# An attention and bilinear FFN block: PSUM banks of the first odd tiles and last down products, values of complete key tiles within the first FFN tile, two reads of plain down products exchanged

## The chip, the cores and the metric

The kernel runs on one core of a Trainium2 chip, in one launch. The metric is the device time of an execution in microseconds; lower is better. TensorE (PE) multiplies into PSUM, eight banks of 128 partitions x 512 fp32; VectorE (DVE) and ScalarE (ACT) read PSUM; GpSimd (POOL) works on SBUF; SyncE's queue (SP) issues the DMAs. Each engine runs its instructions in the order in which the program lists them, and waits on semaphores where it needs another's result.

## The reference

One transformer block in fp32 over 2048 tokens of width 576, with 32 query heads of 18 that share one key and one value head, and an FFN of width 4608 without a nonlinearity:

```python
x = A_x
h = x + _A_ref(_layernorm(x, axis=-1), A_wq, A_wk, A_wv, A_wo)    # softmax(q k^T / sqrt(18)) v, then wo
h2 = h + _B_ref(_layernorm(h, axis=-1), B_w_gate, B_w_up, B_w_down)  # ((x W) * (x V)) W2
```

## The kernel before, in words

**Tiling.** Tokens lie in four blocks b of 512 (NB = 4). Attention works in score pairs (`pair`, L674): two products of keys and queries fill a two-bank PSUM tile "s", ACT takes the exponential into an SBUF tile P (L702). Two pairs complete a key tile of 128 keys; its P tiles wait in the list `pend` until `flush` (L709) multiplies them with V into an accumulator (`values`, L704). In the trace a value product is two PE instructions, so a key tile is eight instructions at L706. 32 pairs make a group of four heads, eight groups a block.

**The FFN.** `ffn(b)` (L1062) runs over 36 tiles f of 128 columns, numbered n_ = 36 b + f. A tile has 27 steps j, nine chunks c of X by three combinations of high and low parts; each step is a gate product into pg and an up product into pu (L1091), in the two halves of the PE array. Behind the steps ACT copies pg into hf (L1125) and DVE multiplies pu into it (L1129). While attention of later blocks is left over (`on`, all of FFN blocks 0 and 1 and the first tiles of block 2), score pairs are dealt among the steps by lists (`PAIRS`, `FIRST` for f = 1, `ENTRY` for n_ = 0: before which step a pair stands), and two more pairs follow an even tile's steps. Behind an even tile, all complete key tiles are flushed and the accumulator is closed: DVE saves it to SBUF (`save`, L719), or turns it when its group is done (L732). Later in the same even tile, from f = 2, comes a down product (`down`, L993) of the pair of tiles before. Block 2's last tiles run without pairs ("off", f from 21); their gate and up banks lie in "s" tiles.

**PSUM.** Tag "s" has two tiles of two banks; "f" has two banks that are taken in turn; "m" and "a" have one bank each. "a" holds the accumulator of the values in the FFN. A new tile on a bank waits for the last reader of the one before. An odd tile usually takes pg in "a" and pu in "f", an even tile pg in "f" and pu in "m"; f = 1 is an exception before, with pg in "f" and pu in "m", and so is the last tile of a block, with pg in "f".

**Down products.** Most pairs of tiles use a seven-product scheme in 14 stages of three matmuls (128 x 288). A stage accumulates onto its bank, and its sum is added into the residual h, either by DVE straight from PSUM (L1045) or by an ACT copy into one of three `tmp` buffers (L1049) that POOL adds (L1050). A later stage on the same bank waits for the read of the one before. `STAGES` is the list while attention is on, `WIDE` the one without it, with four banks. The weights of the next tile are split in the middle of a wide product: DVE's part (L963) stands behind stage 6's read. The last pair of a block (17) has eight plain products y (L1005) of six matmuls each; in blocks 0 and 1 their banks come from `ps_y`, and products with n = 0 are read by DVE (L1015), those with n = 1 by ACT (L1012) and POOL.

**Between blocks.** `spread(b)` transposes the normalised h of the next block (L935), splits it (ACT L940, DVE L941) and copies rows between partition halves by DMA (`X<-X`, L944) for chunks 5 to 8, which steps 15 to 26 read. `both` alternates it with the last down product. SP's queue carries the weights of tiles (`wr`, L953), of down products (`wdo`, L970), the sums' operands and all stores.

Of the kernel before, what the change touches and what calls it, by code (L numbers as in the profile page):

```python
# [57 lines left out]
class Block:  # L58
# [17 lines left out]
        return self.ps.tile([P, TB], F32, tag="m", bufs=1, name=name)  # L76

    def ps_y(self, i, name):
        return self.ps_f(name) if i % 3 else self.ps_m(name)

    def ps_r(self, name):
        self.n_ring += 1
# [979 lines left out]
    def ffn(self, b):  # L1062
        pe, act, dve = self.pe, self.act, self.dve
        X, hid, todo = self.X, [], None
        ahead = self.ahead()
        if b == 0:
            self.sums = self.weight_sums()
            next(self.sums)
        for f in range(NF):
            n_ = NF * b + f  # L1070
            k = f % 2
            w = self.ws.pop(n_)
            on = self.on = self.more(b + 2)
            self.cast_left = self.nc.gpsimd.tensor_copy if on else act.copy
            last = f == NF - 1 and b + 1 < NB
            end = b == NB - 2
            if on:
                pg = (self.ps_a if k and not last and f > 1 else self.ps_f)(f"pg{n_}")
                pu = (self.ps_f if k and f > 1 else self.ps_m)(f"pu{n_}")
            else:  # L1080
                gu = self.ps_s(f"gu{n_}")
                pg, pu = gu[:, 0], gu[:, 1]
            j = 0
            at = FIRST if f == 1 else ENTRY if n_ == 0 else PAIRS[2] if last else PAIRS[k]
            for c in range(9):
                for wk, xk in ((0, 0), (0, 1), (1, 0)):
                    for _ in range(at.count(j)):
                        if on and self.more(b + 2):
                            self.pair()
                    for o, ps in ((0, pg), (64, pu)):  # L1090
                        pe.matmul(ps, w[o:o + 64, wk, c], X[o:o + 64, xk, c], start=(j == 0), stop=(j == 26))  # L1091
                    if j == (8 if on else 2) and todo and not plain(n_ - 2):
                        self.left_sums()
                    if j == (3 if on else 9 if k else 27):
                        self.split_w(n_ + 1)
                    if j == 3 and not on and not k:
                        self.split_w(n_ + 1, (0,))
                    if j == (14 if on else 9 if k else 27):
                        self.load_w(n_ + 2)
                    if j == 5 and k:  # L1100
                        self.left_first(n_ - 1, hid[0])
                    if j == 6 and not k:
                        self.split_wo()
                    if j == (12 if k else 18):
                        self.run_aux(within=True, wo=False)
                    if 0 < f < NF - 1 and j in (8, 16, 24) and self.sums:
                        if next(self.sums, "end") == "end":
                            self.sums = None
                            self.load_wd(self.n_wd + 2)
                    if j == 6 and last and not end:  # L1110
                        self.normal(b + 1)
                    if end and f == TURN - 2 and j == 12:
                        self.normed[NB - 1] = self.mv, self.rstd(self.mv[:, :, 1], "bl", self.nc.gpsimd)
                    if end and f in AHEAD and j in AHEAD[f]:
                        for _ in range(AHEAD[f][j]):
                            next(ahead)
                    j += 1
            if todo and not on:
                for i, _ in enumerate(self.down(b, *todo)):
                    if i == 6:  # L1120
                        self.split_w(n_ + 1, (1,))
                        self.load_w(n_ + 2)
                self.load_wd(self.n_wd + 7)
            hf = self.hh.tile([P, TB], F32, tag="hf", bufs=2, name=f"hf{n_}")
            act.copy(hf, pg)  # L1125
            for _ in range(2 if on and not k else 0):
                if self.more(b + 2):
                    self.pair()
            dve.tensor_tensor(hf, pu, hf, ALU.mult)  # L1129
            hid.append(hf)  # L1130
            if k:
                self.left(n_ - 1, hid)
                hid = []
            if end and f in TURNS:
                for _ in range(TURNS[f]):
                    next(ahead)
            if not k or last:
                self.flush(len(self.pend), True)
            if todo and on:
                for i, _ in enumerate(self.down(b, *todo)):  # L1140
                    if i == 3:
                        self.saved()
                self.load_wd(self.n_wd + 7)
            self.saved()
            if f < NF - 1:
                self.run_aux(wo=k)
            todo = (f // 2,) if k else None
        if end:
            del X, pg, pu, gu, w, ps, hf, self.X
            self.last_block(ahead, self.down(b, *todo))  # L1150
            return
        both(self.spread(b + 1), self.down(b, *todo))
        self.load_wd(self.n_wd + 4)
        if b + 2 < NB:
            self.load_x(b + 2)
# [388 lines left out]
    def run(self):  # L1544
# [105 lines left out]
P1, P2, P3, P4, P5, P6, P7 = (0, 0), (1, 1), (6, 2), (2, 6), (3, 3), (4, 4), (5, 5)  # L1650
# [24 lines left out]
WIDE = [(0, 0, P1, True, (0, 0), False), (1, 2, P1, True, (0, 0), False), (0, 1, P5, True, (1, 1), True),  # L1675
        (1, 3, P5, True, (1, 1), False), (0, 0, P6, False, (0, 1), True), (1, 2, P6, False, (0, 1), False),
        (0, 1, P3, False, (0, 1), True), (1, 3, P3, False, (0, 1), False), (0, 0, P7, False, (1, 1), False),
        (1, 2, P7, False, (1, 1), False), (0, 1, P2, True, (0, 0), True), (1, 3, P2, True, (0, 0), True),
        (0, 0, P4, False, (1, 0), True), (1, 2, P4, False, (1, 0), True)]
LOW, HIGH = [0, 2, 4, 6, 8, 1, 3, 5, 7], [1, 3, 5, 7, 8, 0, 2, 4, 6]  # L1680

# [1 line left out]
def both(a, b):  # L1683

    live = [a, b]
    while live:
        live = [x for x in live if next(x, drain) is not drain]


def plain(n):  # L1690

    return n % NF == NF - 2
# [116 lines left out]
```

## Time and profile before

| what | value |
|---|---|
| three runs | 2266.13, 2270.27, 2272.32 us; median 2270.27 |
| the profiled execution | 2268.11 us, its span 2266.3 us |
| mean granted TensorE clock | 0.998 |
| busiest after PE (share of the span) | PE weight loads 72%, ACT 63%, DVE 61%, POOL 40% |

In the rows of an engine's timeline the first two numbers are start and duration in us, and brackets at the end hold the idle time before and who ended it. Rows of waits have the total in us, the number of times and the longest. A row of windows has a stretch, its length, the busy time (and instructions) of PE, PE weight loads, DVE, ACT and POOL, then the granted clock, the share of the DMA engines and GB/s.

### The profile page before, as it was taken

To read this page: it belongs to the slowest core of one execution; us is meant where nothing else is said; L and a number is where in the kernel's file an instruction comes from. 1 tells how busy PE (TensorE), PEld (TensorE's weight loads), DVE (VectorE), ACT (ScalarE), POOL (GpSimd) and SP (SyncE) were. 2 spreads that over 40 slices of the span, in tenths; PEclk is the share of its full clock that TensorE was granted. 3 is DMA by queue.
4 is the path that set the end of the run, shared out by engine and by line. 5 is a ranking of instruction groups with operands and counts; after the bars stand their busy time and mean duration, and the time that the engine had idled before them with its cause. 6 is when DMAs were issued, how large, how long until landed. Compare 5 with 4: busy or idle time off the path is not lost.

```text
span 2266.3 us, 45964 instructions
## 1 busy us (share of the span) xinstructions
PE 2229.2 (98%) x17972; PEld 1638.3 (72%) x17972; DVE 1371.3 (61%) x2213; ACT 1432.1 (63%) x1941; POOL 897.0 (40%) x972
## 2 busy tenths in 40 slices
PE   7999999999999999999999999999999999999999
PEld 5333345777777777677777777767777788999999
DVE  8565644565556556455555556546455667788776
ACT  7888877656666666566665666665666534555553
POOL 4455401444344444244444435433332454322222
PEclk9999999999999999999999999999999999999999
DMA  5879843455455555555455554564333445677775
GB/s 174 272 256 299 290 138 105 153 171 164 155 168 169 161 183 159 166 158 172 150 173 170 171 160 165 165 201 143 111 123 105 131 162 193 209 244 237 235 249 175
DMA packets 200498, 407.01 MB, mean 180 GB/s; under 512 B 22446, under 2 KB 54318, under 8 KB 200278
## 3 DMA queue, kind: packets, MB, share of 16 engines
q1 hardware_dynamic: 197685, 393.42, 54.2%
q0 software_dynamic: 2592, 10.62, 1.5%
q8 instruction: 143, 2.34, 0.4%
q14 instruction: 78, 0.63, 0.1%
HBM read 317.27 MB, written 74.55 MB: 173 GB/s over the span
## 4 chain that ended last, share of the span: by engine, by line
PE 78%; DMA 2%; DVE 2%; POOL 2%; issue 1%; ACT 1%; SPq 1%; POOLq 0%; ACTq 0%; DVEq 0%
PE pg L1091 19%; PE acc L706 15%; PE y L1039 12%; PE s L701 9%; PE gs L1318 8%; PE pu L1091 5%; PE yq L1283 4%; PE yo L880 3%; PE gs L1325 1%; DMA wr<-in_wgu_dram 1%; POOL h L1050 1%; PE gu L1091 1%; DMA X<-X 1%; DVE ws L963 0%; PE y L1005 0%
## 5 line engine op out<-in xcount | busy, mean ns | idle before, releaser
L702 ACT ACTIVATE P<-s 128x1024 f32<-128x1024 f32 x1024 | 1009.9, 1028 | 229.6 <-PE s L701 145.7
L1091 PE MATMUL pu<-X,ws 64*128 64x512 f32 x2511 | 683.5, 390 | 11.1 <-DVE hf L1129 7.7
L1091 PE MATMUL pg<-X,ws 64*128 64x512 f32 x2511 | 682.8, 390 | 0.0
L1091 PEld LDWEIGHTS pg<-X,ws 64*128 64x128 f32 x2511 | 466.3, 186 | 69.3 <-DMA X<-X 0.9
L1091 PEld LDWEIGHTS pu<-X,ws 64*128 64x128 f32 x2511 | 465.9, 186 | 27.5 <-DVE hf L1129 8.9
L706 PE MATMUL acc<-P,V 128*32 128x512 f32 x4096 | 479.1, 598 | 0.0
L701 PE MATMUL s<-q,kT 56*128 56x512 f32 x2048 | 430.7, 415 | 4.8 <-ACT P L702 3.9
L1050 POOL TENSOR_TENSOR h<-h,tmp 128x288 f32<-128x288 f32 x313 | 251.5, 833 | 331.9 <-ACT tmp L1049 330.0
L1049 ACT COPY tmp<-y 128x288 f32<-128x288 f32 x313 | 125.1, 400 | 342.3 <-PE y L1039 307.4
L701 PEld LDWEIGHTS s<-q,kT 56*128 56x128 f32 x2048 | 201.7, 184 | 170.4 <-ACT P L702 122.2
L1039 PEld LDWEIGHTS y<-wdo,room 128*128 128x128 f32 x2142 | 289.9, 188 | 43.9 <-issue 38.5
L1039 PE MATMUL y<-wdo,room 128*128 128x288 f32 x2142 | 303.8, 300 | 2.4 <-ACT tmp L1049 2.1
L706 PEld LDWEIGHTS acc<-P,V 128*32 128x32 f32 x4096 | 114.6, 109 | 254.8 <-issue 252.0
L1045 DVE TENSOR_TENSOR h<-h,y 128x288 f32<-128x288 f32 x401 | 172.7, 453 | 191.4 <-PE y L1039 191.4
L963 DVE TENSOR_TENSOR ws<-wr,ws 128x1152 fp32r<-128x1152 f32 x108 | 188.6, 1746 | 108.7 <-POOL ws L960 107.3
L1129 DVE TENSOR_TENSOR hf<-pu,hf 128x512 f32<-128x512 f32 x93 | 63.7, 685 | 226.9 <-ACT hf L1125 226.9
L960 POOL CAST ws<-wr 128x1152 fp32r<-128x1152 f32 x108 | 130.8, 1212 | 153.3 <-DMA wr<-in_wgu_dram 136.2
L96 POOL CAST room<-hf 128x256 fp32r<-128x256 f32 (+1 forms) x92 | 58.3, 634 | 320.0 <-DVE hf L1129 320.0
L1266 POOL TENSOR_TENSOR wsum<-wsum,wsum 128x512 f32<-128x512 f32 x72 | 146.3, 2032 | 42.5 <-DMA wsum<-in_wgs_dram 37.0
L1091 PE MATMUL gu<-X,ws 64*128 64x512 f32 x810 | 94.5, 389 | 0.0
L97 DVE TENSOR_TENSOR room<-hf,room 128x256 fp32r<-128x256 f32 (+1 forms) x108 | 91.9, 851 | 3.4 <-ACT room L96 1.9
L1091 PEld LDWEIGHTS gu<-X,ws 64*128 64x128 f32 x810 | 78.3, 184 | 13.9 <-issue 0.7
(268 smaller groups left out, 2762.4 us busy)
## 6 DMA issues: line engine op xcount, KB each, us to landing
wdo<-wd_dram SPq DMA_DIRECT2D x492, 288.0 KB
wr<-in_wgu_dram SPq DMA_DIRECT2D x108, 576.0 KB
wsum<-in_wgs_dram SPq DMA_DIRECT2D x108, 256.0 KB
wd_dram<-wd_room SPq DMA_DIRECT2D x20, 1008.0 KB
wsum_dram<-wsum SPq DMA_DIRECT2D x72, 256.0 KB
raw<-wsum_dram SPq DMA_DIRECT2D x72, 256.0 KB
q<-q_dram SPq DMA_DIRECT2D x64, 216.0 KB
raw<-in_wgs_dram SPq DMA_DIRECT2D x54, 256.0 KB
```

The lines of the kernel that those rows point to most:

```text
L701: self.pe.matmul(s_[:, i], self.kT[o:o + 56, t * P:(t + 1) * P], q[o:o + 56, pr], start=True, stop=True)
L702: self.act.activation(p_, s_, AF.Exp, scale=SCALE)
L706: self.pe.matmul(acc[32 * j:32 * j + 32, :], self.V[:, t, :], Ps[j // 2][:, j % 2, :], start=first, stop=last, skip_group_check=True)
L960: self.nc.gpsimd.tensor_copy(w[:, 0], self.wr[n])
L963: self.dve.tensor_tensor(w[:, 1], self.wr.pop(n), f32(w[:, 0]), ALU.subtract)
L1039: pe.matmul(y[:, :HD], m[:, t * P:(t + 1) * P], k, start=(first and j == 0), stop=(j == 2), skip_group_check=True)
L1045: dve.tensor_tensor(hs, hs, y[:, :HD], ALU.add)
L1049: act.copy(z, y[:, :HD])
L1050: pool.tensor_tensor(hs, hs, z, ALU.add)
L1091: pe.matmul(ps, w[o:o + 64, wk, c], X[o:o + 64, xk, c], start=(j == 0), stop=(j == 26))
L1266: pool.tensor_tensor(to, x, y, op)
L1318: pe.matmul(bank[:, g * HT:(g + 1) * HT], W[:, wk, c, g], X[:, 2 * xk + c], start=(first and g == c == wk == xk == 0), stop=(c == 1 and wk ...
```

## The change

Four edits:

- `ps_y`: of the eight plain products of a block's last down product, the numbers 1, 4 and 7 take bank "m" and the others "f"; before, 0, 3 and 6 took "m".
- `ffn`: the tile f = 1 takes its banks as the other odd tiles do, pg in "a" and pu in "f"; before, pg in "f" and pu in "m".
- `ffn`: in the very first tile (n_ = 0) the values of all complete key tiles are multiplied ahead of step 21; before, all of them stood behind the tile.
- `WIDE`: stage 9's sum is read by DVE and stage 11's by ACT and POOL; before, the other way round.

```diff
     def ps_y(self, i, name):
-        return self.ps_f(name) if i % 3 else self.ps_m(name)
+        return self.ps_m(name) if i % 3 == 1 else self.ps_f(name)
...
             if on:
-                pg = (self.ps_a if k and not last and f > 1 else self.ps_f)(f"pg{n_}")
-                pu = (self.ps_f if k and f > 1 else self.ps_m)(f"pu{n_}")
+                pg = (self.ps_a if k and not last else self.ps_f)(f"pg{n_}")
+                pu = (self.ps_f if k else self.ps_m)(f"pu{n_}")
...
                         if on and self.more(b + 2):
                             self.pair()
+                    if n_ == 0 and j == 21:
+                        self.flush(len(self.pend))
                     for o, ps in ((0, pg), (64, pu)):
...
-        (1, 2, P7, False, (1, 1), False), (0, 1, P2, True, (0, 0), True), (1, 3, P2, True, (0, 0), True),
+        (1, 2, P7, False, (1, 1), True), (0, 1, P2, True, (0, 0), True), (1, 3, P2, True, (0, 0), False),
```

## The prediction

> **What bounds the kernel now.** I read the first lines of the page, then who waited for whom on TensorE, then the order of time of each engine around every wait that the change can touch.
>
> ```profile
> span 2266.3 us, 45964 instructions
> PE 2229.2 (98%) x17972; PEld 1638.3 (72%) x17972; DVE 1371.3 (61%) x2213; ACT 1432.1 (63%) x1941; POOL 897.0 (40%) x972
> PE 78%; DMA 2%; DVE 2%; POOL 2%; issue 1%; ACT 1%; SPq 1%; POOLq 0%; ACTq 0%; DVEq 0%
> PE pu L1091 <- DVE hf L1129: 7.7, 3, 3.8
> PE pu L1091 <- DMA X<-X: 3.4, 4, 1.3
> PE y L1039 <- ACT tmp L1049: 2.1, 4, 0.5
> ```
>
> TensorE is the bound: 98% busy, 78% of the last chain. The change removes no matmul, so it can only win TensorE's waits (the last three lines: microseconds, times, longest), what follows a wait in a lower clock, or lose by new ones. These three kinds sum to 13.2 us, and the edits aim at them; other waits, at the kernel's start above all, aren't touched.
>
> **First odd tiles (f = 1 of blocks 0, 1, 2).** Before, pu of tile 0 and pu of tile 1 both lie in the one bank "m"; worse, tile 2's pu wants "m" too, while tile 1, an odd tile, has no value products behind it to cover the eviction.
>
> ```profile
> 383.64 0.39 PE L1091 MATMUL pg<-X,ws 64*128 64x512 f32 x1
> ...
> 390.98 0.61 PE L1091 MATMUL pg<-X,ws 64*128 64x512 f32 x2
> 393.53 0.50 PE L1091 MATMUL pu<-X,ws 64*128 64x512 f32 x1 [1.93 <-DVE hf L1129]
> ...
> 940.31 0.39 PE L1091 MATMUL pg<-X,ws 64*128 64x512 f32 x1
> 944.52 0.79 PE L1091 MATMUL pu<-X,ws 64*128 64x512 f32 x1 [3.82 <-DVE hf L1129]
> ...
> 949.75 0.40 PE L1091 MATMUL pu<-X,ws 64*128 64x512 f32 x1
> ...
> 1497.82 0.39 PE L1091 MATMUL pg<-X,ws 64*128 64x512 f32 x1
> 1500.13 0.50 PE L1091 MATMUL pu<-X,ws 64*128 64x512 f32 x1 [1.93 <-DVE hf L1129]
> 944.50:949.70 5.20, 5.18 (x24) 4.15 (x26) 3.54 (x6) 1.91 (x2) 1.60 (x2) 0.50 0.26 53
> ```
>
> From the first pg of tile 1 (383.64) to its last (390.98) lie 26 product pairs and six score pairs, 7.34 us, 0.23 us a step. The second pg in the 390.98 row is tile 2's first, issued at 391.21; its pu starts only at 393.53. The stalls are therefore 393.53 - 391.21 = 2.3, 944.52 - 940.31 = 4.2 and 1500.13 - 1497.82 = 2.3 us. After the longest one the window row grants a clock of 0.50: from 944.52 to 949.75 stand ten products and two score pairs, 12 x 0.23 = 2.8 us of work in 5.2, so another 2.4 us. With pu in "f", tile 2's "m" was freed a whole tile earlier and these go: 2.3 + 6.6 + 2.3 = 11.2 us.
>
> What is added: tile 1's pg now needs bank "a", which the value products held until DVE has saved (or turned) the accumulator.
>
> ```profile
> 383.21 0.72 DVE L732 STREAM_TRANSPOSE os<-acc 128x512 f32<-128x512 f32 x1 [5.36 <-PE acc L706]
> ...
> 932.30 0.69 DVE L719 TENSOR_TENSOR ob<-ob,acc 128x512 f32<-128x512 f32 x1 [2.98 <-PE acc L706]
> ...
> 932.73 0.39 PE L1091 MATMUL pg<-X,ws 64*128 64x512 f32 x1
> ```
>
> DVE ends at 383.93 and 932.99; pg started at 383.64 and 932.73, behind two score pairs that cover the rest. So 0.3 us in blocks 0 and 1; behind it in TensorE's queue stand the whole tile's products. In block 2 an output projection's 24 products stand between (the aux list of tile 0's end) and cover it: nothing. Without that cover a block would pay 0.8 us.
>
> Then what is late next? In block 1, tile 2 gains 6.6 - 0.3 = 6.3 us, but its own hf product on DVE doesn't move with it:
>
> ```profile
> 952.05 1.15 POOL L960 CAST ws<-wr 128x1152 fp32r<-128x1152 f32 x1 [5.85 <-DMA wr<-in_wgu_dram]
> ...
> 953.23 2.16 DVE L963 TENSOR_TENSOR ws<-wr,ws 128x1152 fp32r<-128x1152 f32 x1 [5.16 <-POOL ws L960]
> ...
> 957.06 0.68 DVE L1129 TENSOR_TENSOR hf<-pu,hf 128x512 f32<-128x512 f32 x1
> ...
> 1508.49 0.69 DVE L1129 TENSOR_TENSOR hf<-pu,hf 128x512 f32<-128x512 f32 x1
> 955.59 7.00 PE acc L706 x64
> ```
>
> The landing of the weights (POOL casts them at 952.05, after 5.85 us of waiting) sets DVE's in-order queue up to the hf product's end at 957.74, which releases "m", the bank of the first down product's second stage. The down product, behind the value products at 955.59 + 7.00 = 962.6 now, would start at 956.3, and that stage 0.4 us later (a fourteenth of the 6.17 us quoted below), at 956.7: it waits 1.1 us. Block 1 keeps 5.2. In block 2, tile 2 would begin at 1497.82 and take 35 steps of 0.23 with its scores, 8.1 us, then 7.0 of values: its down product comes at 1512.9, 3.7 us behind the hf product's end at 1509.18 (the second row). I take block 0 as block 2. So this edit: 2.3 - 0.3 + 5.2 + 2.3 = 9.5.
>
> **Values within the first tile.** Before, five key tiles are accumulated behind tile 0 of block 0, while inside it TensorE waits for the copies of X.
>
> ```profile
> 371.82 0.39 PE L1091 MATMUL pu<-X,ws 64*128 64x512 f32 x1
> ...
> 373.44 0.50 PE L1091 MATMUL pu<-X,ws 64*128 64x512 f32 x1 [0.69 <-DMA X<-X]
> ...
> 375.69 0.50 PE L1091 MATMUL pu<-X,ws 64*128 64x512 f32 x1 [0.59 <-DMA X<-X]
> ...
> 377.70 5.43 PE L706 MATMUL acc<-P,V 128*32 128x512 f32 x40
> 376.20:379.60 3.40, 3.40 (x19) 1.28 (x21) 0.69 (x1) 2.52 (x3) 0.00 (x0) 0.50 0.94 355
> 1497.80:1501.20 3.40, 1.47 (x13) 0.89 (x12) 1.75 (x3) 1.55 (x3) 0.80 (x1) 1.00 0.36 83
> 367.16 5.61 ACT L702 ACTIVATE P<-s 128x1024 f32<-128x1024 f32 x6 [0.17 <-PE s L701]
> 377.44 1.94 ACT L702 ACTIVATE P<-s 128x1024 f32<-128x1024 f32 x2 [0.32 <-PE s L701]
> ```
>
> The row at 371.82 is step 20; step 21 is where the new flush stands. Three key tiles are then complete (ACT made their tiles in the x6 row), 24 of the 40 products; at 7.00 / 64 = 0.109 us each they last 2.6 us, from 372.05 to 374.7. Steps 21 to 23 and a score pair, 0.9 us, bring TensorE to 375.6, when the last copy lands (375.69). So the 2.6 us cost nothing, and are gone from behind the tile. Tile 0 still ends at about 376.4; what is left, two key tiles, waits for two exponentials (0.97 each) behind the hf copy: about 379.2, plus the last products and DVE's 0.72 us on the accumulator: pg of tile 1 at about 380.6, where 383.64 + 0.3 would have stood. Gain 3.0 against before, the 0.3 above included; I therefore count 3.3 here. No DMA and no other queue is passed: the flush issues TensorE products alone.
>
> The clock is a term of its own. The two window rows above show 0.50 for 3.4 us after waits of only 0.69 and 0.59, and 1.00 around the 1.93 of 1500.13. The gaps that I leave, about 1.2 us near 379 and 1.1 us at 957, could each bring 3.4 us at half clock, 1.7 us lost; I take nothing, as nearer to the second row (a single gap, products dense on both sides), and keep 3.4 for the range. [...]
>
> **Last down products (pair 17 of blocks 0 and 1).** Bank "m" goes from products 0, 3, 6 to 1, 4, 7. Either way product i waits for the read of product i - 3, so the order of waits inside stays. At the end, the next tile's pu takes "m" behind product 7 (read by ACT) instead of 6.
>
> ```profile
> 918.97 0.50 PE L1091 MATMUL pu<-X,ws 64*128 64x512 f32 x1
> ...
> 919.13 0.40 ACT L1012 COPY tmp<-y 128x288 f32<-128x288 f32 x1 [1.19 <-PE y L1005]
> ...
> 926.31 0.50 PE L1091 MATMUL pu<-X,ws 64*128 64x512 f32 x1 [0.86 <-DMA X<-X]
> ```
>
> A new wait of 919.53 - 918.97, 0.6 us, with tile 0's products queued behind. But the same tile waits 0.86 us for its last X copy at 926.31, which hides it: nothing. Without that cover it is 1.2 us for both blocks.
>
> **Two reads exchanged (seven plain down products).** Stage 9's read goes to DVE, stage 11's to ACT and POOL.
>
> ```profile
> L1045 DVE TENSOR_TENSOR h<-h,y 128x288 f32<-128x288 f32 x401 | 172.7, 453 | 191.4 <-PE y L1039 191.4
> 1803.25 6.17 PE L1039 MATMUL y<-wdo,room 128*128 128x288 f32 x42
> 1807.05 1.78 DVE L963 TENSOR_TENSOR ws<-wr,ws 128x1152 fp32r<-128x1152 f32 x1
> ...
> 1866.18 5.42 PE L1039 MATMUL y<-wdo,room 128*128 128x288 f32 x39
> 1869.63 1.35 DVE L963 TENSOR_TENSOR ws<-wr,ws 128x1152 fp32r<-128x1152 f32 x1
> 1871.67 0.40 ACT L1049 COPY tmp<-y 128x288 f32<-128x288 f32 x1 [1.17 <-POOL h L1050]
> ```
>
> In the last four, stage 13 waits 0.53 us for ACT's read of stage 9, itself late for POOL. DVE is free at 1870.98, has read by 1871.43, and stage 13 comes at 1871.60: 2.1 us gained. In the first three DVE is busy until 1808.83 and would have read at 1809.28, while stage 13 comes at 1803.25 + 13 x 0.44 = 1809.0: 0.3 to 0.45 us new, 1.3 us lost. Net 0.8; bounds 2.1 and -1.3. Stage 11's bank isn't wanted again within the product, so its later read holds nobody.
>
> **Sum.** 9.5 + 3.3 + 0.8 + 0 = 13.6 us off the profiled execution (2268.1 us, of which 2266.3 are the span): 2254.5. The median of the runs shown is 2.2 us above it, so I forecast a median of 2256.7.
>
> **Rivals.** (1) The gain is handed back: what I found in block 1, weights landing no earlier, holds in full in blocks 1 and 2, and only block 0 and the reads keep theirs: 2.0 + 3.3 + 0.8 = 6.1, a median of 2264.2. For it, DVE's queue waits for POOL and the DMA in all three blocks; against it, the slack that I count. (2) Slower: DVE's release of "a" is late at the three starts of tile 1, because something stands ahead of it in DVE's queue. Each start pays the wait w and, as after 944.52, 2.4 us of half clock. The change ends slower from 3 (w + 2.4) = 13.6, w = 2.1 us; at w = 4.2, the longest stall of this sort now, it is 6.2 us slower, 2276.5. Against it: DVE starts on the accumulator 0.1 us after its last product (377.70 + 5.43 to 383.21), and sat idle 5.36 and 2.98 us before. (3) The edit of the banks does nothing, because pu's wait is for another reason than "m": then 3.3 + 0.8 - 0.6 = 3.5, 2266.8. Against it: pg of the same step went ahead, and pu started 0.06 us after DVE's hf product.
>
> **How the numbers follow.** Forecast 0.82, rival 1 0.11, rival 2 0.03 (taken whole as slower), rival 3 0.04. A measurement here tells about 0.3%, 6.8 us, from no change: 2263.5. Best end: reads at 2.1 (+1.3), no wait at 957 (+1.1), and the profiled execution's 2.2 below the median: 2252.1. Worst end within the forecast: two half-clock windows (3.4), last down products uncovered (1.2), reads at -1.3 (2.1): 2263.4; the range goes on to rival 1's 2264.2 and leaves out rivals 2 and 3. Faster is the forecast's 0.82, same rivals 1 and 3 with 0.15, slower 0.03.
>
> **What would show it.** The wait of pu for hf (7.7) gone; none above 0.8 us at pg of tile 1; a wait of about 1 us of y on DVE's hf in block 1's first down product; 24 value products before step 21 of the first tile and 16 behind it; pu of tile 0 waiting 0.6 us for ACT's tmp in blocks 1 and 2, with the wait for X shorter by as much; the 0.53 waits gone, three smaller ones on DVE's h in their place; clock 1.00 near 376 and 947. The prediction is wrong if pg of tile 1 waits over 2 us, or if the wins are there and later waits have grown by as much.

## The result, and the profile after

| kernel | executions | median us | lowest to highest | ratio to before, 95% interval |
|---|---|---|---|---|
| before | 6 | 2268.40 | 2265.92 to 2272.32 | |
| after | 6 | 2254.93 | 2252.57 to 2256.76 | 0.9939, 0.9927 to 0.9952 |

Faster by 13.5 us, 0.6%, twice the 0.3% that a measurement tells from nothing. The forecast median of 2256.7 lies 1.8 us above the measured one, because the median of before was 2270.27 in the three runs shown and is 2268.40 in six. The profiled execution of after took 2255.83 us with a span of 2254.0.

First the page of the kernel after: its span, the engines' busy time, and TensorE's share of the chain that ended last.

```profile
span 2254.0 us, 45956 instructions
PE 2226.0 (99%) x17972; PEld 1632.7 (72%) x17972; DVE 1373.7 (61%) x2213; ACT 1431.2 (63%) x1941; POOL 898.1 (40%) x972
PE 83%; DVE 1%; DMA 1%; ACT 1%; POOL 0%; issue 0%; SPq 0%; ACTq 0%; DVEq 0%; POOLq 0%
```

The number of matmuls is the same; the chain's share on TensorE went from 78% to 83%, so what was won is waiting. Next, who waited for whom on TensorE from 360 to 2200 us (total, times, longest):

```profile
PE pu L1093 <- DMA X<-X: 3.0, 2, 1.7
PE s L701 <- ACT P L702: 1.4, 2, 1.0
PE y L1039 <- DVE h L1045: 1.0, 3, 0.4
PE yo L880 <- ACT tmp L884: 0.5, 1, 0.5
PE pg L1093 <- DVE os L732: 0.2, 1, 0.2
PE pg L1093 <- DVE ob L719: 0.2, 1, 0.2
```

The wait of pu for hf (7.7 us) and that of the down products for ACT's tmp (2.1) are gone. New are the two 0.2 us at pg of tile 1, the three on DVE's h, and 1.0 us at a score pair (the other 0.4 of that row lies at 360.6, ahead of the first tile). (Lines of after stand two further down: L1093 was L1091, L1131 was L1129.)

TensorE's timeline of after at the places that the prediction names:

```profile
373.81 2.78 PE L706 MATMUL acc<-P,V 128*32 128x512 f32 x24
...
378.87 3.11 PE L706 MATMUL acc<-P,V 128*32 128x512 f32 x16
...
382.89 0.47 PE L1093 MATMUL pg<-X,ws 64*128 64x512 f32 x1 [0.24 <-DVE os L732]
...
915.77 0.49 PE L1093 MATMUL pu<-X,ws 64*128 64x512 f32 x1
...
923.29 0.50 PE L1093 MATMUL pu<-X,ws 64*128 64x512 f32 x1 [1.26 <-DMA X<-X]
930.12 0.47 PE L1093 MATMUL pg<-X,ws 64*128 64x512 f32 x1 [0.23 <-DVE ob L719]
...
946.94 0.50 PE L701 MATMUL s<-q,kT 56*128 56x512 f32 x2 [0.99 <-ACT P L702]
947.37 7.07 PE L706 MATMUL acc<-P,V 128*32 128x512 f32 x64
954.37 1.79 PE L1039 MATMUL y<-wdo,room 128*128 128x288 f32 x10
```

24 value products now lie inside the first tile and 16 behind it. The first down product of block 1 starts at 954.37 and runs without the wait for bank "m" that the prediction had put there (the row shows the first ten of its 42 matmuls); instead the last score pair of tile 2 waits 0.99 us before the values. And the windows of after around the first tile and block 1's tile 2:

```profile
376.20:379.60 3.40, 3.40 (x30) 1.95 (x26) 0.54 (x1) 2.18 (x3) 0.00 (x0) 1.00 1.05 353
945.00:949.70 4.70, 3.71 (x36) 1.42 (x36) 0.29 (x1) 3.19 (x5) 0.47 (x1) 1.00 0.76 227
```

Both are at a granted clock of 1.00; before granted 0.50 in the same places.

**Where the time went.** The span is cut at the same instructions in both traces: the first pg, and in each block the first product of the first down product, of the transposes of `spread`, and of the values behind them. Each entry is the difference of two starts, minus that of before.

| stretch | forecast | after |
|---|---|---|
| first pg to first down product, block 0 | -5.3 | -4.73 |
| transposes to first values, block 1 (the last down product and tile 0) | 0 | 0.00 |
| first values to first down product, block 1 | -5.2 | -5.13 |
| transposes to first values, block 2 | 0 | -0.01 |
| first values to first down product, block 2 | -2.3 | -2.26 |
| FFN without attention (the wide down products) | -0.8 | -2.10 |
| kernel's start to first pg | 0 | +1.65 |

The other stretches differ by 0.2 or less. The code ahead of the first pg is the same in both kernels, and its length differs by up to 4.1 us among the profiles of this study, so the +1.65 is no effect of the change. Without it the difference is 13.9 us.

### The profile page after: what moved, and what is told of

Read it like the earlier page. It is cut to its first block, busy times and chain, and to the rows that moved or that the text cites. A ratio compares the mean times of both kernels' runs of the same rounds, so it can differ in the third digit from the quotient of the medians.

```text
span 2254.0 us, 45956 instructions
## 1 busy us (share of the span) xinstructions
PE 2226.0 (99%) x17972; PEld 1632.7 (72%) x17972; DVE 1373.7 (61%) x2213; ACT 1431.2 (63%) x1941; POOL 898.1 (40%) x972
## 3 DMA queue, kind: packets, MB, share of 16 engines
q8 instruction: 143, 2.34, 0.4%
## 4 chain that ended last, share of the span: by engine, by line
PE 83%; DVE 1%; DMA 1%; ACT 1%; POOL 0%; issue 0%; SPq 0%; ACTq 0%; DVEq 0%; POOLq 0%
PE pg L1093 18%; PE acc L706 15%; PE y L1039 13%; PE s L701 9%; PE gs L1320 8%; PE pu L1093 7%; PE yq L1285 4%; PE gu L1093 4%; PE yo L880 3%; PE gs L1327 2%; DMA X<-X 1%; PE y L1005 0%; PE tx L935 0%; ACT P L702 0%; POOL h L1050 0%
## 5 line engine op out<-in xcount | busy, mean ns | idle before, releaser
L1093 PE MATMUL pu<-X,ws 64*128 64x512 f32 x2511 | 680.5, 389 | 3.2 <-DMA X<-X 3.0
L1093 PE MATMUL pg<-X,ws 64*128 64x512 f32 x2511 | 680.4, 389 | 0.5 <-DVE os L732 0.2
L1093 PEld LDWEIGHTS pg<-X,ws 64*128 64x128 f32 x2511 | 465.0, 185 | 66.2 <-issue 2.5
L1093 PEld LDWEIGHTS pu<-X,ws 64*128 64x128 f32 x2511 | 464.5, 185 | 25.3 <-DMA X<-X 3.8
L701 PE MATMUL s<-q,kT 56*128 56x512 f32 x2048 | 425.2, 414 | 5.7 <-ACT P L702 5.0
L1131 DVE TENSOR_TENSOR hf<-pu,hf 128x512 f32<-128x512 f32 x93 | 63.7, 685 | 225.6 <-ACT hf L1127 225.6
L96 POOL CAST room<-hf 128x256 fp32r<-128x256 f32 (+1 forms) x92 | 58.2, 633 | 315.1 <-DVE hf L1131 315.1
L97 DVE TENSOR_TENSOR room<-hf,room 128x256 fp32r<-128x256 f32 (+1 forms) x108 | 94.1, 871 | 3.4 <-ACT room L96 1.8
L1093 PE MATMUL gu<-X,ws 64*128 64x512 f32 x810 | 94.5, 389 | 0.0
L1093 PEld LDWEIGHTS gu<-X,ws 64*128 64x128 f32 x810 | 78.6, 184 | 13.5 <-issue 1.5
```

The source lines that it names most:

```text
L701: self.pe.matmul(s_[:, i], self.kT[o:o + 56, t * P:(t + 1) * P], q[o:o + 56, pr], start=True, stop=True)
```

## The experiments

The medians of before beside which each ratio stands are 2268.0 us (first four kernels), 2270.19 (next four) and 2267.03 (last three). A gain in microseconds is the ratio's, and the ratio is not the quotient of two medians (2268.0 - 2258.61 would be 9.4 us where the ratio gives 8.6). The rows of waits are taken from the same 360 to 2200 us.

**The banks of f = 1 alone.** On the kernel before:

```diff
-                pg = (self.ps_a if k and not last and f > 1 else self.ps_f)(f"pg{n_}")
-                pu = (self.ps_f if k and f > 1 else self.ps_m)(f"pu{n_}")
+                pg = (self.ps_a if k and not last else self.ps_f)(f"pg{n_}")
+                pu = (self.ps_f if k else self.ps_m)(f"pu{n_}")
```

> The banks of the first odd tiles alone (pg of f = 1 in a, pu in f). My theory, that tile 2's pu waited for bank m: the waits of pu for hf (7.7 us) go in all three blocks with the half clock behind the longest, pg of tile 1 waits 0.2 to 0.3 us in blocks 0 and 1, and block 1 hands back about 1 us before its first down product. Between the first step of the FFN and the first down product of a block it gains 2.0 in block 0, 5.1 in block 1, 2.3 in block 2: 9.4 us in all, a ratio near 0.9959. Rival, the gain is handed back at the first down product: 2 us in all. Rival, the banks do nothing and the waits stay: 0, or 0.6 us slower.

Measured: 2258.61 us, ratio 0.9962 (0.9948 to 0.9977), 8.6 us. TensorE's waits:

```profile
PE pu L1091 <- DMA X<-X: 3.5, 4, 1.3
PE y L1005 <- DVE h L1015: 1.4, 2, 0.7
PE s L701 <- ACT P L702: 1.0, 1, 1.0
```

The stall on hf is gone with this edit alone, the waits for X and of the last down product stand, and the score pair's wait comes with it. By stretch it wins 3.44 us in block 0, 5.19 in block 1 and 2.04 in block 2, and 0.01 in the wide products.

**The values within the first tile alone.** On the kernel before:

```diff
+                    if n_ == 0 and j == 21:
+                        self.flush(len(self.pend))
```

> The values of complete key tiles ahead of step 21 of the first tile, alone. My theory, that they fill the wait for the copies of X: block 0 gains 2.4 to 3.3 us between its first step and tile 1's first pg, the granted clock stays at 1.00 near 376, and nothing else moves. The waits of pu for hf remain 7.7 us. Rival, the values only push step 21 back and the tile ends later by as much: 0.

Measured: 2267.95 us, ratio 0.9994 (0.9984 to 1.0004), 1.4 us and inside the interval of nothing. TensorE's waits:

```profile
PE pu L1093 <- DVE hf L1131: 7.9, 3, 4.0
PE pu L1093 <- DMA X<-X: 2.2, 2, 1.3
```

Of the four waits for X two are left, 1.2 us less; block 0's stretch is 2.79 us shorter. The difference between the two is the clock, as the accounting below shows.

**The two reads alone.** The last part of the diff on the kernel before (stage 9 True, stage 11 False).

> The two reads exchanged, alone. My prediction's term: the four waits of 0.53 us go, three new waits of 0.3 to 0.45 us on DVE come, 0.8 us gained over the seven down products. The changed kernel's trace gives 2.1 us over the same stretch; if that is the edit's own, this run shows 2.1, and if it is a late effect of the other edits, 0.8.

Measured: 2266.88 us, ratio 0.9988 (0.9977 to 0.9999), 2.7 us; the wide stretch is 2.16 us shorter. Its waits from 1780 to 1940 us:

```profile
PE yo L880 <- ACT tmp L884: 0.8, 1, 0.8
PE y L1039 <- DVE h L1045: 0.5, 2, 0.3
```

The 2.1 us behind ACT are gone and two small waits on DVE's h have come; one wait for ACT's tmp at an output projection grew from 0.5 to 0.8 us.

**The last down products alone.** On the kernel before:

```diff
-        return self.ps_f(name) if i % 3 else self.ps_m(name)
+        return self.ps_m(name) if i % 3 == 1 else self.ps_f(name)
```

> The banks of the last down products alone. My theory: no gain and no loss, since what it changes lies ahead of a wait for the copies of X: the wait of product 5 for DVE (0.7 us, twice) goes, pu of the next tile waits 0.6 us for ACT's read of product 7, and the wait for X grows by what is left over. The time from the first transposition of a block to its first value products stays within 0.1 us. Rival: the 0.7 us are won outright, 1.4 us in all.

Measured: 2268.93 us, ratio 1.0001 (0.9992 to 1.0010). The stretches from the transposes to the first values differ from before by -0.01 us in both blocks. Nothing, as forecast; but inside, two terms cancel (below). This profile also showed something about the clock. Its rows: a wait and two windows.

```profile
395.78 0.79 PE L1091 MATMUL pu<-X,ws 64*128 64x512 f32 x1 [1.93 <-DVE hf L1129]
```

```profile
395.80:399.20 3.40, 3.40 (x16) 2.74 (x18) 2.37 (x5) 1.03 (x1) 1.48 (x2) 0.50 0.90 296
376.20:379.60 3.40, 2.15 (x11) 1.02 (x11) 0.00 (x0) 1.41 (x2) 0.00 (x0) 1.00 1.06 245
```

Here the 1.93 us stall of block 0 is followed by 3.4 us at half clock (0.50, the first window); in before the same stall was not (1.00 from 395.80 to 399.20), and the window at half clock (0.50 from 376.20 to 379.60) lay behind the small waits for X of 0.69 and 0.59 us.

**pu alone to "f".** On the kernel before, only the second line of the first experiment (pu of f = 1 to "f"; pg stays in "f").

> Of the first odd tiles' banks only pu's moves: pu of f = 1 in f, pg stays in f. Theory, that tile 2's wait was for bank m: that wait goes, but tile 2's pg now falls on tile 1's pg, which ACT copies before DVE multiplies. From before's rows ACT's copy ends 1.6, 1.9 and 1.6 us after tile 2's first step could have begun, against 2.3, 4.2 and 2.3 for DVE: a gain of 0.7, about 4.7 (the half clock of 2.4 goes too) and 0.7, some 6 us. Rival, that the move of pg to a is what helps: 0.

Measured: 2264.48 us, ratio 0.9976 (0.9965 to 0.9986), 5.4 us. Its waits, and the granted clock behind the longest of them (941.04, 1.81 us):

```profile
PE pg L1091 <- ACT hf L1125: 4.8, 3, 1.8
```

```profile
941.70:945.10 3.40, 3.40 (x20) 3.08 (x18) 3.26 (x8) 1.29 (x2) 1.21 (x2) 0.50 0.06 16
```

The wait moves from pu to pg: with both tiles of f = 1 in the two "f" banks, tile 2's pg takes over the bank of tile 1's pg, which ACT is still copying. It is 4.8 us instead of 7.7, because ACT's copy comes before DVE's product of the same hf. By stretch it wins 2.24, 3.07 and 0.15 us in the three blocks where 0.7, 4.7 and 0.7 were expected: in block 0, 1.7 us of it are the half clock near 376 in before, which lies ahead of this edit, and in block 1 half clock (0.50 from 941.70 to 945.10) came behind the 1.81 us too, where it had been expected to go. That the total lies near the 6 us expected is luck.

**pg alone to "a".** On the kernel before, only the first line (pu stays in "m").

> Of the first odd tiles' banks only pg's moves: pg of f = 1 in a, pu stays in m. Theory, that tile 2's wait was for bank m: the waits of pu for hf stay (7.7 us, or 7.1 where tile 1 starts later), pg of tile 1 waits 0.3 us in blocks 0 and 1: 0 to 0.6 us slower. Rival, that the move of pg is what helps: some 9 us faster.

Measured: 2269.54 us, ratio 0.9997 (0.9988 to 1.0006). Its waits:

```profile
PE pu L1091 <- DVE hf L1129: 6.8, 3, 2.9
```

The bank "m" is still tile 2's, and nothing is won. Rival 3 of the prediction (another reason than "m") falls with these two: the wait follows the bank, to pg and ACT when pu leaves "m", and stays when only pg leaves.

**After, the chunk of the output projection put behind tile 2.** What does the score pair wait for? ACT's timeline in after (the first row is the read of the last down product's product 7, used further below):

```profile
915.32 0.40 ACT L1012 COPY tmp<-y 128x288 f32<-128x288 f32 x1 [1.33 <-PE y L1005]
...
943.52 1.03 ACT L702 ACTIVATE P<-s 128x1024 f32<-128x1024 f32 x1
945.34 0.62 ACT L96 CAST room<-ob 128x512 fp32r<-128x512 f32 x1 [0.79 <-DMA ob<-ob]
945.87 1.02 ACT L702 ACTIVATE P<-s 128x1024 f32<-128x1024 f32 x1
946.78 0.58 ACT L1127 COPY hf<-pg 128x512 f32<-128x512 f32 x1
```

Between the exponentials of 943.52 and 945.87 stands a cast (L96), part of the chunk that `run_aux` takes up at step 18 of tile 2. It waits 0.79 us for a DMA of `ob`, and the exponential behind it frees "s" late. Taking the step away from that place, so that it runs with the tile's end:

```diff
-                    if j == (12 if k else 18):
+                    if j == (12 if k else 18) and n_ != NF + 2:
                         self.run_aux(within=True, wo=False)
```

> The changed kernel, with the step of the aux list that stands at step 18 of tile 2 of block 1 left for the tile's end: ACT's and DVE's split of the attention output, which waits for a DMA, then stands behind the score pairs and the hf product. Theory, that this copy in ACT's order delays the last score pair by 0.99 us: that wait goes, and the first down product starts up to 1 us earlier, unless my prediction's other limit, bank m behind DVE's hf product, takes its place. If that limit binds alone, nothing is gained; DVE's hf product should come some 0.6 us earlier too, since its part of the split stands behind it. Expected: 0.5 to 1.0 us earlier between the block's first transposition and its first down product.

Measured: 2261.37 us, ratio 0.9962 (0.9948 to 0.9976), some 5 us worse than after by the two ratios (after 0.9939). The score wait is gone and the first down product starts 1.24 us earlier, counted from the values behind tile 0. But TensorE's timeline of this kernel goes on with

```profile
969.60 1.06 PE L880 MATMUL yo<-wos,room 128*128 128x288 f32 x6 [1.50 <-DVE hf L1131]
973.39 3.67 PE L880 MATMUL yo<-wos,room 128*128 128x288 f32 x15 [2.73 <-DVE h L887]
```

and from 973.2 to 976.6 the clock is 0.50. I had overlooked where the chunk's products go: they now came in a place where they need banks that DVE had not read, and the stretch up to the next block's transposes is 7.1 us longer than in after. The theory of the cast stands (no cast, no wait), the edit was a poor one.

**After, the chunk right behind tile 2's hf product.** The same, but with the step put back one place later:

```diff
             dve.tensor_tensor(hf, pu, hf, ALU.mult)
+            if n_ == NF + 2:
+                self.run_aux(within=True, wo=False)
```

> The changed kernel, with the aux step of tile 2 of block 1 (ACT's and DVE's split of the attention output) put right behind that tile's hf product instead of ahead of step 18. Theory, that this copy in ACT's order holds the last score pair for 0.99 us: that wait goes as it went when the step was put at the tile's end, but the output projection behind the first down product finds its operands and doesn't wait. From the block's first value products to its first down product 1.0 to 1.3 us less than in the changed kernel, and none of it given back up to the next block. Rival, that the projection or bank m takes the time back in any case: 0.

Measured: 2256.11 us, ratio 0.9948 (0.9933 to 0.9963). TensorE's timeline at the first down product of block 1:

```profile
954.07 0.66 PE L1039 MATMUL y<-wdo,room 128*128 128x288 f32 x3
955.15 1.06 PE L1039 MATMUL y<-wdo,room 128*128 128x288 f32 x6 [0.42 <-DVE hf L1131]
956.92 2.28 PE L1039 MATMUL y<-wdo,room 128*128 128x288 f32 x15 [0.70 <-DVE h L1045]
```

The score wait is won (1.27 us from the values behind tile 0 to here), and at once the wait appears that the prediction had named, the down product's second stage behind DVE's hf product; with the 0.70 behind it, where DVE now has the chunk's split (L97) ahead of its read, the following stretch is 1.26 us longer than in after. What is won is handed back within 0.01 us.

**After, one key tile of values before step 24 of tile 0 in blocks 1 and 2.** Can the first tile's trick also cover the two waits for X that are left (1.26 and 1.72 us)?

```diff
+                    if f == 0 and b in (1, 2) and j == 24:
+                        self.flush(1)
```

> The changed kernel, and in blocks 1 and 2 one complete key tile is multiplied ahead of step 24 of tile 0, where pu waits 1.26 and 1.66 us for the copies of X. Theory, that values fill such a wait for nothing: those waits shrink by 0.87 us each (eight products of 0.109), eight products fewer stand behind the tile, 0.9 us per block, 1.7 us in all. Rival, that the shorter rest behind the tile waits for the exponentials: 0.

Measured: 2257.21 us, ratio 0.9940 (0.9926 to 0.9953), no different from after. TensorE's timeline of block 2:

```profile
1472.68 0.50 PE L1095 MATMUL pu<-X,ws 64*128 64x512 f32 x1 [1.71 <-DMA X<-X]
1473.81 1.06 PE L706 MATMUL acc<-P,V 128*32 128x512 f32 x8
```

The eight products stand behind the wait instead of ahead of it: the step was chosen wrongly, by three. In block 1 this kernel shows one more thing. Tile 1 starts 0.7 us later than in after, ACT's cast then has no wait for `ob`, and the last score pair waits 0.17 us instead of 0.99; yet the exponential behind the cast starts at 945.72 (945.87 in after), and the first down product at 954.22 (954.37). A shorter wait is no gain here: the work ahead of it had only come later.

**After, both: values before step 21, the chunk behind the hf product.** The two edits above, with j == 21.

> As the kernel with the step behind the hf product, and one complete key tile multiplied ahead of step 21 (not 24, which lies behind the wait) of tile 0 in blocks 1 and 2. Theory: the waits of pu for the copies of X shrink from 1.26 and 1.72 by 0.87 us each, and the three key tiles left behind the tile still cover the exponentials: 0.9 us per block, with 1.0 to 1.3 from the moved step 2.7 to 3.0 us less than the changed kernel from the first FFN step to the end, about 0.12%. Rival, that block 1 hands its part back at the first down product: 1.8 to 2.1.

Measured: 2255.65 us, ratio 0.9942 (0.9928 to 0.9955). Its timeline:

```profile
955.43 2.82 PE L1039 MATMUL y<-wdo,room 128*128 128x288 f32 x18 [0.62 <-DVE hf L1133]
...
1471.27 1.06 PE L706 MATMUL acc<-P,V 128*32 128x512 f32 x8
1473.05 0.49 PE L1095 MATMUL pu<-X,ws 64*128 64x512 f32 x1 [0.29 <-DMA X<-X]
```

The waits for X are covered (0.29 of 1.72 is left in block 2, less than a listed wait in block 1), but block 1 then waits 0.62 us for DVE's hf, and in block 2 an output projection waits 0.47 us for DVE's h. From the transposes to the first down product block 1 wins 1.8 us more than after did, block 2 wins 0.3 less, and 0.85 us of block 1's gain comes back in its next stretch.

**After, once more**, beside these two on the same chip.

> The changed kernel once more, beside the two others on the same chip: a ratio of 0.994 to the kernel before, the same stretches as in its first profile to 0.1 us, and no half clock unless a wait above 1 us happens to meet a window of it.

Measured: 2255.26 us, ratio 0.9940 (0.9926 to 0.9953). So neither of the two kernels built on after is measurably faster than after. Two executions of one kernel also differ in the wide stretch; here the first three wide products, in after and then in after once more:

```profile
1799.07 0.66 PE L1039 MATMUL y<-wdo,room 128*128 128x288 f32 x3 [0.34 <-DVE h L1045]
...
1821.46 0.66 PE L1039 MATMUL y<-wdo,room 128*128 128x288 f32 x3 [0.41 <-DVE h L1045]
...
1843.54 0.66 PE L1039 MATMUL y<-wdo,room 128*128 128x288 f32 x3 [0.23 <-DVE h L1045]
```

```profile
1799.77 0.66 PE L1039 MATMUL y<-wdo,room 128*128 128x288 f32 x3 [0.23 <-DVE h L1045]
...
1816.21 5.88 PE L1039 MATMUL y<-wdo,room 128*128 128x288 f32 x42
...
1838.03 5.88 PE L1039 MATMUL y<-wdo,room 128*128 128x288 f32 x42
```

Three waits in the one, one in the other; its wide stretch is 3.30 us shorter than before's, against 2.10, where the same to 0.1 us had been expected.

## Why the prediction was right, and where its steps were off

**The sum.** 13.6 us forecast, 13.5 us by the medians, 13.9 by stretches. The ratios of the four parts alone give 8.6 + 1.4 + 2.7 - 0.2 = 12.5 us, each within 2 to 3 us either way: within that the parts add up, and no sign of one needing another is seen. That the sum came out within 0.1 us is partly luck: by stretch block 0 gave 0.6 us less than forecast and the reads 1.3 more, and a 3.4 us window of half clock near 376 in the profiled execution of before was counted as part of the gain.

**First odd tiles (9.5).** Right in mechanism and size: 8.6 us alone (5.2 to 11.8); by stretch 10.7, of which 1.7 is the half clock near 376, ahead of the edit. The release of "a" costs 0.24 and 0.23 us where 0.3 was put; rival 2 needed 2.1. Block 1 kept 5.13 us where 5.2 was put, but not for the reason given. The step said "The landing of the weights ... sets DVE's in-order queue up to the hf product's end at 957.74", with 1.1 us of waiting for "m". DVE's rows of after:

```profile
950.41 2.16 DVE L963 TENSOR_TENSOR ws<-wr,ws 128x1152 fp32r<-128x1152 f32 x1 [5.13 <-POOL ws L960]
...
954.23 0.68 DVE L1131 TENSOR_TENSOR hf<-pu,hf 128x512 f32<-128x512 f32 x1
```

From the end of the weight split to the end of the hf product pass 954.91 - 952.57 = 2.34 us, as before (957.74 - 955.39 = 2.35): DVE's queue does hang on the weights, as the step says. Counted from the block's first transpose (909.29 before, 906.26 after) the hf product ends after 48.45 and 48.65 us, so it did not move with the tile either. But another wait came first: on ACT's queue the cast of `ob` held the last exponential, the values started 0.99 us late, and the down product with them, so that its second stage, some 0.4 us behind 954.37, found "m" all but free at 954.91. Take that wait away, and "m" is waited for (0.42 and 0.62 us in the two kernels that did). So two limits lie behind one another within a microsecond, and the step had found the second of them. It looked for what is late next on DVE, whose bank it followed, and not on ACT, whose exponentials the same tile also waits for. That both limits cost about the same, 1 us, is luck, and with it the 5.2.

**Values within the first tile (3.3).** 2.41 + 0.24 = 2.65 in the profile (the start of tile 1's pg, 17.95 us behind the first pg in before, 15.54 in after, and its wait). The size was taken from a profile in which 3.4 us stood at half clock, and that belongs to the execution, not to the place: of six profiles with the same code there, four are at 1.00. Taking block 0 apart with the waits and the clock of each trace:

| kernel | waits for X gone | hf stall gone | half clock against before | new wait | sum | measured |
|---|---|---|---|---|---|---|
| after | 1.28 | 1.93 | 1.7 | -0.24 | 4.67 | 4.73 |
| banks alone | 0 | 1.93 | 1.7 | -0.3 | 3.33 | 3.44 |
| values alone | 1.28 | 0 | 1.7 | 0 | 2.98 | 2.79 |
| reads alone | 0 | -0.07 | 0 | 0 | -0.07 | -0.04 |
| last products alone | 0 | 0 | 1.7 - 1.7 | 0 | 0 | 0.03 |

The 1.7 us are an estimate, half of the 3.4 us at 0.50 (376.20 to 379.60 in before, 395.80 to 399.20 in last products alone). Banks alone has no edit at all ahead of tile 1, keeps waits of 0.69 and 0.61 us for X, and shows no half clock at 376 either (1.00 from 376.20 to 379.60). So this part is worth 1.3 us of waits, and 1.7 more only in executions whose clock drops there; alone, it measured 1.4 (-0.9 to 3.6).

**Clock (0 taken).** Right for this kernel: no window of after's profile at these places is below 1.00, though waits of 0.99, 1.26 and 1.7 us stand in it. The reason given, that a single gap with dense products around it costs nothing, is not supported: the single 1.93 of block 0 in the kernel with the last products alone was followed by half clock (0.50 from 395.80 to 399.20), and so was the 1.81 with pu alone in "f" (0.50 from 941.70 to 945.10). The longer stalls of block 1 had half clock behind them as well: 0.50 behind 3.82 us in before (944.50 to 949.70), 4.0 with the values alone (945.60 to 949.00) and 4.24 with the last products alone (948.70 to 952.10).

**Last down products (0).** The net was right, a step inside it was wrong: "Either way product i waits for the read of product i - 3". The two banks of "f" are not always taken in turn: in the program as built, with "m" at 1, 4 and 7, product 5 lies on product 3's bank, which ACT has read long before, and no longer on product 2's, which DVE reads and which product 6 now takes. The rows of 0.7 us (y L1005 behind DVE's h, 1.4 in two blocks, still there with the banks alone) are gone in after. Tile 0's pu does start late behind product 7, ACT having ended at 915.72 (its copy L1012 of 0.40 us from 915.32) and pu at 915.77. The waits for X grew from 0.86 to 1.26 in block 1 and from 1.30 to 1.72 in block 2, where the prediction had them shorter, and hide it all: 0.00 and -0.01 us.

**Reads exchanged (0.8).** The term that was mis-sized most: 2.16 alone, 2.10 in after, and 1.81 to 3.30 in the five further profiles that hold it. From the start of each product to the start of what follows it, the last four gain 2.66 in after (2.1 put), and the first three lose 1.29 (1.3 put), of which 0.98 are the waits on DVE's h. What the working left out are the two output projections behind the first two (L880): they take 0.73 less. And the loss is not fixed: in after once more only one of the three waits came, and the same three products lost 0.02. The working had set a read at DVE's end in one execution against a start of TensorE in the same; one execution gives no fixed order of the two. What moves them from one execution to the next is not shown.

**Rivals.** Rival 1 didn't hold: all three blocks kept their gain. Its mechanism is real one step further on: the 1.27 us that the moved chunk won beyond after came back as 1.26. Rival 2 fell with the 0.24 and 0.23 us at pg, rival 3 with the two kernels that moved one bank each.

## What to carry to other kernels

When a stall is removed, list what is late next on every engine that the next stage passes, not only on the engine that held the bank: here the in-order queue of ACT, with a cast that waits 0.79 us for a DMA, came a microsecond ahead of DVE's, and removing it only uncovered DVE's. A tile that changes bank moves the waits of all tiles that share the tag; write out the bank of each, in the program as built, before saying who waits for whom. And a term read from one profiled execution should be taken apart into waits and clock: here the waits for X in the first tile came in all six profiles of the same code (0.57 to 0.69 us each), half clock behind them in two (0.50 and 0.54 from 376.20 to 379.60).

## What the runs showed of the hardware

**Short waits and half clock.** Before and the five kernels built on it without the values' edit have the same code in the first tile of block 0, and waits of 0.67 to 0.69 and 0.57 to 0.61 us for the copies of X there. Two of these six profiles show half clock from 376 on (from 376.20 to 379.60 before has 0.50, reads alone 0.54), four don't show it behind those waits (1.00 in that stretch and from 379.00 to 383.00). The stall of 1.93 to 2.01 us in block 0 stands in before, values alone, reads alone, last products alone and pg alone, and only in last products alone did half clock follow (0.50 from 395.80 to 399.20, where the other four have 1.00).

Two stretches of 3.41 us around the stall of block 0, first in last products alone, then in before:

```profile
392.36:395.77 3.41, 1.49 (x13) 0.90 (x9) 0.70 (x2) 2.52 (x4) 0.00 (x0) 1.00 0.36 73
395.77:399.18 3.41, 3.40 (x16) 2.75 (x18) 2.40 (x5) 1.03 (x1) 1.47 (x2) 0.50 0.90 294
```

```profile
389.88:393.29 3.41, 1.72 (x15) 1.11 (x11) 0.51 (x1) 2.75 (x4) 0.00 (x0) 1.00 0.66 170
393.29:396.70 3.41, 3.17 (x28) 2.76 (x30) 3.34 (x6) 1.73 (x2) 2.49 (x3) 1.00 0.85 258
```

In last products alone TensorE is idle for 3.41 - 1.49 = 1.92 us in the first row, at 1.00, and the second row is at 0.50; in before it is idle for 1.69 us in the first row and 0.24 in the second, and both are at 1.00. So a stall of the same length in the same code had half clock behind it in one execution and not in another; no run here tests what sets the two apart. Nor do the waits that were measured give a length at which the clock falls: 0.50 stood behind 0.69 and 0.59 us in before, behind 1.81 with pu alone and behind 1.93 in last products alone, and 1.00 behind 1.93, 2.00 and 2.01 in before, reads alone and pg alone. In before half clock lasted 3.42 us the first time (376.22 to 379.64) and 6.82 the second, from within the stall of 3.82 on (942.84 to 949.66).

The longest wait left in after, 1.72 us in block 2, stands at 1.00, as does all of after's profile from 360 to 2200 us. As for the spread of the times, 29 executions of before beside the first four kernels spread from 2264.49 to 2275.78 us, with mean granted clocks of 0.995 to 0.999, the eleven of after over 2252.57 to 2256.76, with 0.999 to 1.000.
